# A new order table for a fused attention and gated-MLP kernel: the second batch in bf16, constants on GpSimd, more unread matmuls, more crossings by DMA

## The chip, the cores and the metric

The kernel runs on one core of one Trainium2 chip. The metric is device microseconds of one execution. The core has five engines, each with its own queue that it works off in order: PE (TensorE: matmuls and transposes, results in the eight banks of PSUM), DVE (VectorE), ACT (ScalarE), POOL (GpSimd) and SP (SyncE, which here only issues DMAs). ACT and POOL issue DMAs too; POOL's are written by its software and can change the type on the way, SP's and ACT's are not.

## The reference

Two stages. First a linear attention over q, k, v of 8 batches x 8 heads x 576 tokens x 64, with a feature map of 2 x 128 features; then a gated MLP (512 to 1024, halved, mixed over the tokens, back to 512) over the attention's output.

```python
def phi(x):
    proj = np.einsum('bhsd,df->bhsf', x, w_phi)
    proj = proj - np.max(np.abs(proj), axis=-1, keepdims=True)
    return np.concatenate([np.exp(proj), np.exp(-proj)], axis=-1)
q_p, k_p = (phi(q), phi(k))
kv = np.einsum('bhsf,bhsd->bhfd', k_p, v)
z = np.sum(k_p, axis=2)
num = np.einsum('bhsf,bhfd->bhsd', q_p, kv)
den = np.einsum('bhsf,bhf->bhs', q_p, z)[..., None] + 1e-06
return (num / den).astype(np.float32)
...
h = np.maximum(x @ w_in, 0.0)
u, v = (h[..., :d_ff // 2].copy(), h[..., d_ff // 2:].copy())
v_n = (v - mu) / np.sqrt(var + 1e-06)
v_s = np.einsum('ts,bsd->btd', w_spatial, v_n) + b_spatial[None, :, None]
gated = u * v_s
return (gated @ w_out).astype(np.float32)
```

## The kernel before

The 576 tokens of a batch are four blocks of 128 and a tail of 64. The tails of two batches make one tile of 128, so there are eight batches and four groups of tails (group g holds batches 2g and 2g+1).

The order of all work is one long string, `ORDER`. A word such as `tk.1.0.1:0` or `vs.0.0.0:0@V` names an operation and its numbers (batch, half of the heads or block, part), behind the colon the PSUM banks or buffers it takes, and behind the @ the engine (A for ACT, V for DVE, P for POOL, S for SP; the words of PE have none). A loop at the kernel's end reads the words and issues each as it comes; nothing is reordered afterwards. Each engine so gets its words in the string's order, and an instruction waits only for what it reads and for buffers to come free.

The operations that matter here:

- `lkf`, `lqf` (batch 0) and `lkg`, `lqg` (batch 1) load k and q as fp32 into buffers that other tiles use later (`ob`, `uT`, `vn`, `xT`), issued on ACT or SP. `lk`, `lq` load later batches into `ld` as bf16, issued on POOL. `lkt`, `lqt` load a group's tails as fp32 into `tf` on SP, and `ckt`, `cqt` cast them on POOL into `tl`; `lkb`, `lqb` load them as bf16 on POOL.
- `tk`, `tq` turn four 128 x 128 blocks of k or q on PE (line 505), and `tkc`, `tqc` copy the result from PSUM to `T`. Later batches cross by `xk`, `xq`, a DMA transpose on SP (line 488). Tails: `tkt`, `tqt` on PE (line 549) and `xkt`, `xqt` by DMA (line 536).
- `kp`, `qp` are projections (line 574), `km`, `qm` their maxima over the features on DVE (line 579), `ke` the exponentials of k on ACT (line 583), `kem`, `kemw` those of its maxima (line 588), `vs`, `vst` the products of v with them (lines 629 and 641), `kv` the products of keys and values on PE (lines 659 and 661).
- The maxima of q have to be subtracted along the other axis. `qs` splits them into two bf16 parts on POOL (lines 674 and 675, into `mhl`), and they cross either by `qt`, a transpose on PE (line 679), and the copy `qc`, or by `qd`, a DMA transpose on SP (line 725). `qf` reads them (`mT`, line 689) and `qe` takes the exponential (line 694).
- `warm` is a number of matmuls of the identity with itself whose result nobody reads (line 361).
- `cident2`, `csel`, `csel2`, `chalf`, `zmhl`, `zvnt` set up constants: the bf16 identity, a selector, an exponent, cleared or filled buffers.
- The MLP: `vm`, `vr`, `vb`, `va`, `vw`, `vn` (lines 849 to 875), `um`, `ur` (line 917), `sm`, `sg` (lines 931 to 940), `om`, `oc`, `od` (line 946, a copy from PSUM to `ob`, and the output's DMA on SP). `omh`, `och`, `odh` do one output tile in two halves (line 965).

```python
def qd(e, b, cc, hg):
    nc.sync.dma_start_transpose(out=get("mT", (b, cc, hg)), in_=at["mhl", (b, cc, hg)])
...
def lk(e, b):
    nc.gpsimd.dma_start(out=get("ld", ("k", b)), in_=main_ap(k, b, 0, H))
...
def warm(e, n):
    place = places.pop(0)
    for i in range(n):
        nc.tensor.matmul(out=bank(place)[:, 3 * P:4 * P], lhsT=ident, rhs=ident, start=True, stop=True)
```

In `turn`, which `tk` and `tq` call, a batch that has no `ld` buffer is turned from its fp32 tile with the fp32 identity, and one that has is turned in bf16.

## Time and profile before

| | us |
|---|---|
| three runs | 267.02, 266.33, 265.49 |
| their median | 266.33 |
| the profiled execution | 267.15 |
| its span, first to last instruction | 265.4 |
| PE busy | 246.8 |
| DVE busy | 218.5 |
| ACT busy | 197.8 |
| POOL busy | 177.8 |

The profile names each group of instructions by line, engine, operation, and output and input tiles. Matmuls are pipelined: one of 128 columns lasts about 0.22 us, while several in a row start far closer together, so a short gap between two matmuls can hide in the busy time. Some matmul records can be missing. PEclk is the clock that the chip grants PE, in tenths or as a share of the full one. A wait names the engine, the line that waited, and what came last before it could go on. POOL's instructions that issue DMAs stand in its queue like others.

### The profile page before, as it was taken

What the parts mean: (1) busy time and instruction counts of PE and PEld (TensorE: products, weight loads), DVE (VectorE), ACT (ScalarE), POOL (GpSimd) and SP (SyncE); (2) the same over time, 40 slices, a digit from 0 to 9 for tenths busy, and PEclk for the clock granted to TensorE, in tenths of its full rate; (3) what the DMA queues carried; (4) which work ended last, traced back from release to release, by engine and by line L of the source; (5) the groups of instructions that cost most, each with busy time, mean ns of one, the idle gap of its engine ahead of it and who ended that gap; (6) DMA issues with size and microseconds to landing.
All of it is one profiled execution on the core that took longest, in us unless ns stands there. A gap on an engine that the chain in (4) does not pass through costs nothing. (4 is left out here: it accounts for less than half of the span.)

```text
span 265.4 us, 8226 instructions
## 1 busy us (share of the span) xinstructions
PE 246.8 (93%) x3305; PEld 156.5 (59%) x3341; DVE 218.5 (82%) x371; ACT 197.8 (75%) x319; POOL 177.8 (67%) x322
## 2 busy tenths in 40 slices
PE   4787799999999999999999989999999999999993
PEld 4666577756555567465556656455546665546441
DVE  4799969998799999998999958999998768594550
ACT  2799669999979999989898778898779736412033
POOL 4029989699999983879999891269988911556000
PEclk9999869999999999999999999999999999999999
DMA  6999999993699969899999899896900670003546
GB/s 174 343 287 290 218 194 211 239 102 22 125 235 191 159 159 168 221 190 141 188 179 247 134 146 210 172 155 145 308 23 0 86 166 2 1 2 132 149 143 212
DMA packets 82682, 42.92 MB, mean 162 GB/s; under 512 B 51538, under 2 KB 78034, under 8 KB 82644
## 3 DMA queue, kind: packets, MB, share of 16 engines
q1 hardware_dynamic: 61700, 30.98, 53.7%
q0 software_dynamic: 18512, 9.05, 27.7%
q10 hardware_dynamic: 2432, 2.36, 2.9%
q8 instruction: 26, 0.43, 0.6%
q14 instruction: 12, 0.10, 0.1%
HBM read 32.82 MB, written 9.44 MB: 159 GB/s over the span
## 5 line engine op out<-in xcount | busy, mean ns | idle before, releaser
L694 ACT ACTIVATE qf<-banks 128x1024 bf16<-128x1024 f32 x72 | 70.4, 1027 | 9.3 <-PE banks L689 8.3
L629 POOL TENSOR_TENSOR vs<-v,em 128x512 bf16<-128x512 f32 x61 | 63.2, 1052 | 7.2 <-ACT em L588 6.8
L583 ACT ACTIVATE kf<-banks 128x1024 bf16<-128x1024 f32 x64 | 63.7, 1042 | 4.1 <-PE banks L574 1.8
L579 DVE TENSOR_REDUCE mq<-banks 128x8 f32<-128x1024 f32 x36 | 43.4, 1216 | 3.4 <-PE banks L574 2.7
L579 DVE TENSOR_REDUCE mk<-banks 128x8 f32<-128x1024 f32 x32 | 38.6, 1213 | 1.2 <-PE banks L574 0.7
L917 PE MATMUL banks<-xT,w_u 128*128 128x512 bf16 x128 | 32.4, 379 | 0.1
L931 PE MATMUL banks<-w_spT,vn 128*128 128x512 bf16 x117 | 31.7, 379 | 0.7 <-issue 0.2
L849 PE MATMUL banks<-w_v,xT 128*128 128x512 bf16 x116 | 31.3, 379 | 0.7
L273 ACT COPY ob<-banks 128x512 f32<-128x512 f32 (+1 forms) x25 | 14.3, 591 | 21.5 <-PE banks L946 21.5
L946 PE MATMUL banks<-w_out,uT 128*128 128x512 bf16 x114 | 29.6, 379 | 0.5 <-issue 0.2
L940 DVE TENSOR_TENSOR uT<-banks,uT 128x512 bf16<-128x512 f32 x32 | 21.5, 682 | 7.4 <-PE banks L933 7.3
L279 ACT ACTIVATE vr<-banks 128x512 bf16<-128x512 f32 (+1 forms) x28 | 16.8, 606 | 11.4 <-PE banks L849 9.6
L659 PE MATMUL banks<-vs,kf 128*128 128x66 bf16 x512 | 24.5, 194 | 0.9 <-POOL vs L629 0.8
L859 POOL TENSOR_SCALAR vn<-vr,mv,rs 128x512 bf16<-128x512 bf16 x32 | 24.4, 772 | 0.9
L659 PEld LDWEIGHTS <-kf 128*128 128x128 bf16 x512 | 22.1, 98 | 4.8 <-issue 2.3
L755 DVE TENSOR_TENSOR x<-banks,rc 128x512 bf16<-128x512 f32 x32 | 22.1, 690 | 1.2 <-DVE rc L750 0.2
L574 PE MATMUL banks<-wphi,T 64*128 64x128 bf16 x512 | 22.4, 217 | 0.5 <-ACT tT L273 0.2
L871 DVE BATCH_NORM_STATS2 st<-vr 128x6 f32<-128x512 bf16 x32 | 21.4, 683 | 1.5 <-ACT vr L279 1.2
L661 PE MATMUL banks<-vst,kft 128*128 128x66 bf16 x128 | 21.3, 192 | 1.3 <-POOL vst L641 1.3
L744 PEld LDWEIGHTS <-qf 128*128 128x128 bf16 x512 | 19.0, 97 | 4.4 <-issue 0.8
L744 PE MATMUL banks<-kv,qf 128*128 128x66 bf16 x512 | 20.9, 193 | 0.3 <-DVE mq L579 0.2
L574 PEld LDWEIGHTS <-T 64*128 64x128 bf16 x512 | 15.6, 94 | 7.6 <-issue 5.8
(131 smaller groups left out, 470.5 us busy)
## 6 DMA issues: line engine op xcount, KB each, us to landing
v<-in_v_dram SPq DMA_DIRECT2D x16, 512.0 KB, 5.1
out_dram<-ob SPq DMA_DIRECT2D x31, 256.0 KB, 2.9
ld<-in_q_dram POOLq DMA_DIRECT2D x6, 512.0 KB, 8.1
ld<-in_k_dram POOLq DMA_DIRECT2D x6, 512.0 KB, 8.2
ob<-in_k_dram ACTq DMA_DIRECT2D x4, 256.0 KB, 4.6
uT<-in_q_dram ACTq DMA_DIRECT2D x2, 512.0 KB, 10.4
vn<-in_k_dram SPq DMA_DIRECT2D x2, 512.0 KB, 8.3
vt<-in_v_dram SPq DMA_DIRECT2D x8, 128.0 KB, 7.3
```

The costliest lines, as they stand in the source:

```text
L574: nc.tensor.matmul(out=bank(banks[y])[:, n * F:(n + 1) * F], lhsT=xT[halves[y], n, :], rhs=wphi[halves[y], :], start=True, stop=True)
L579: nc.vector.tensor_reduce(out=out_, in_=pp.rearrange("p y (n f) -> p y n f", f=F), axis=AX.X, op=ALU.max, apply_absolute_value=True)
L583: nc.scalar.activation(out=kf[:, s].rearrange("p y n f -> p y (n f)"), in_=pp, func=AF.Exp, bias=0.0, scale=(1.0, -1.0)[s])
L629: ENG[e].tensor_tensor(out=get("vs", (b, j))[:, s, :, 0:D], in0=at["v", (b, j // 2)][:, (j % 2) * n:(j % 2 + 1) * n, :], in1=at["em", (b, ...
L659: nc.tensor.matmul(out=pv[:, hh, s, :], lhsT=kf[:, s, c % 2, 2 * hh + c // 2, :], rhs=w[:, s, NB * hh + c, :], start=(c == 0), stop=False)
L694: nc.scalar.activation(out=at["qf", u][:, s].rearrange("p y n t -> p y (n t)"), in_=at["pq", u], func=AF.Exp, bias=0.0, scale=(1.0, -1.0)[s])
L744: nc.tensor.matmul(out=at["pn", u][:, y, n, :], lhsT=f[:, s, y, n, :], rhs=at["kv", b][:, hg * HH + n, s, :], start=(s == 0), stop=(s == 1))
L849: nc.tensor.matmul(out=bank(place)[r], lhsT=lhs[:, kc, r], rhs=w_v[:, kc, :], start=(kc == 0), stop=(kc == KC - 1))
L859: ENG[e].tensor_scalar(out=out_, in0=in_, scalar1=mv, scalar2=rs, op0=ALU.add, op1=ALU.mult)
L917: nc.tensor.matmul(out=bank(place).rearrange("p (c t) -> p c t", c=NB), lhsT=w_u[:, kc, dc * P:(dc + 1) * P], rhs=at["xT", b][:, :, kc, :] ...
L931: nc.tensor.matmul(out=bank(place), lhsT=at["vn", b][:, c, cs], rhs=w_spT[:, c, 0:T0], start=(c == 0), stop=False)
L946: nc.tensor.matmul(out=bank(place), lhsT=at["uT", b][:, dc, c * P:(c + 1) * P], rhs=w_out[:, dc, :], start=(dc == 0), stop=(dc == KC - 1))
```

## The change

The string is another one. It has 1436 words for 1417, and almost none stands where it stood. What differs beside the order:

- Batch 1's k and q are loaded as bf16 by POOL (`lk.1`, `lq.1` for `lkg`, `lqg`), so that their 32 transposes on PE are of bf16. Batch 0 stays fp32.
- The tails of group 1 are loaded as bf16 by POOL (`lkb.1`, `lqb.1` for `lkt.1`, `lqt.1`, `ckt.1`, `cqt.1`) and cross by DMA (`xkt.1`, `xqt.1`), as groups 2 and 3 did; group 0 stays on PE.
- The maxima of batches 2 and 3 cross by DMA (eight `qd` for eight `qt` and eight `qc`), as those of batches 4 to 7 did.
- `cident2`, `csel`, `csel2`, `chalf` and two `zmhl` move from DVE to POOL, one `zvnt` to POOL and one to ACT. Three `vs` move from DVE to POOL. Copies from PSUM are dealt out anew between ACT and DVE, among them 15 `ur`.
- 233 unread matmuls in 43 words for 95 in 10: 28 of the words are of five: 25 stand among the first batches' work and three at the very end.
- On SP the bias `lbs` and the first tail of k are issued first, and one quarter of batch 0's k (`lkf.2`) moves there from ACT.
- The last output tile is a whole one (`om.7.0`); the tile in halves stands before it.

```diff
 ORDER = """
-cident@P lphi@S lkf.3:1@A zvst.0@P cident2@V warm.21:0 zmhl.0@V lqt.0:0@S csel@V lkf.0:3@A chalf@V csel2@V lkf.1:0@A
-zmhl.3@V zmhl.2@P zmhl.1@P lqf.0:1@A lkg.0:0@S lkg.1:1@S lkf.2:2@A lkt.0:1@S tk.0.1.1:4 warm.3:0 lqf.1:0@A tk.0.0.0:5
-warm.4:0 ctab@A tkc.0.0.0:1@V tk.0.0.1:6 warm.9:0 tkc.0.0.1@A cphi@V kp.0.0:0,1 tkc.0.1.1:0@A kp.0.1:2,3 ke.0.0.1:0@A
-km.0.1:0@V kp.0.3:6,7 tq.0.0.0:4 warm.10:5 ke.0.0.0@A km.0.3:1@V lvt.0:0@S ke.0.1.0:1@A tk.0.1.0:5 tqc.0.0.0:2@V
-lv.0.0:0@S ke.0.1.1@A tkc.0.1.0@V tq.0.0.1:4 warm.5:5 km.0.0@V tqc.0.0.1@A ke.0.3.0:2@A lqg.1:0@S qp.0.0.0:2,3
-kp.0.2:4,5 qm.0.0.0:3@V tk.1.0.1:0 ke.0.3.1@A tq.0.1.0:1 tkc.1.0.1:1@V tqc.0.1.0:0@A tq.0.1.1:2 lqg.0:1@S tk.1.0.0:3
...
-qr.1.1.0:1@V lv.4.0:3@S qx.1.1.0@V lk.4:1@P qt.2.0.1:2 vm.1.0:7 vrt.0.1:0@A txc.1.1@V vs.2.1.1:3@P vbt.0.1:3@V
...
-sm.7.1:5 sg.6.3@V sg.6.1@V sm.7.0:2 sg.7.1@V om.6.0:5 sg.7.0@V sg.7.3@V om.6.1:1 oc.6.0:2@A od.6.0@S om.7.2:7
-oc.6.1:1@A od.6.1@S omh.7.3.0:3 oc.7.2:3@A om.7.0:6 och.7.3.0:0@V od.7.2@S odh.7.3.0@A om.6.3:7 oc.7.0:4@A om.6.2:4
-od.7.0@S oc.6.3:2@A od.6.3@S om.7.1:1 oc.6.2:1@A od.6.2@S omh.7.3.1 oc.7.1:3@A och.7.3.1@A od.7.1@S odh.7.3.1@A
+cident@P lbs:0@S lkf.0:0@A cident2@P warm.23:0 lphi@S chalf@P zmhl.2@P ctab@A zmhl.3@P zmhl.0@P lkt.0:1@S zsp@P
+zmhl.1@P lk.1:0@P lkf.2:4@S lkf.1:2@A lvt.0:0@S lkf.3:1@A zvnt.0@P tk.0.0.0:4 warm.3:0 lqf.0:1@A lv.0.0:3@S warm.5:7
+warm.1:0 tkc.0.0.0:0@V zvnt.1@A warm.5:2 warm.3:0 csel@P cphi@V warm.5:7 warm.7:0 spb@P kp.0.0:6,7 warm.5:4
+ke.0.0.1:0@A tk.0.0.1:3 warm.15:0 tkc.0.0.1@V ke.0.0.0@A warm.5:3 warm.5:0 lqf.1:2@A km.0.0:0@V tk.0.1.1:1 warm.5:0
+warm.5:4 tkc.0.1.1:1@V warm.5:2 kp.0.1:4,5 ckt.0:0@P kp.0.3:6,7 warm.5:3 km.0.1@V lv.0.1:1@S ke.0.3.1:2@A zvst.0@P
+tkt.0:3 warm.5:2 warm.5:2 tktc.0:0@A km.0.3:1@V warm.5:0 warm.5:1 ke.0.1.0:1@A tk.0.1.0:1 csel2@P tq.0.0.0:3 lqt.0:0@S
+ke.0.3.0@A tkc.0.1.0@V lq.1:1@P tq.0.0.1:2 warm.5:0 tqc.0.0.0:2@V tqc.0.0.1@A tk.1.0.0:7 lsp:0@P tk.1.1.0:3
+kem.0.1:0@A tkc.1.0.0:3@V kem.0.0@A tk.1.1.1:2 lspt:1@P ke.0.1.1@A tkc.1.1.0:5@V tk.1.0.1:0 qp.0.1.0:6,7 warm.5:1
+tkc.1.0.1@V lq.2:2@P qm.0.1.0:2@V tkc.1.1.1@A kp.0.2:0,1 tq.0.1.0:4 ke.0.2.1:3@A vsz.0.0:0@P lk.2:0@P warm.5:5
+tqc.0.1.0:4@V qp.0.0.0:6,7 warm.5:3 ke.0.2.0@A lv.1.0:2@S qm.0.0.0:1@V qs.0.1.0:0@P kpt.0:4,5 lv.1.1:0@S lin.0@P
...
+qd.2.1.0:2@S qf.1.1.0:6,7 qe.1.1.1.0:3@A txc.1.0:1@V vn.0.3@P kp.2.1:2,3 sm.0.1:0 km.2.1@V qd.2.0.1:1@S qe.1.1.1.1@A
...
+oc.7.2:4@A od.7.2@S om.5.3:0 oc.5.1:1@A od.5.1@S om.6.1:7 oc.5.3:0@V om.6.3:6 od.5.3@S oc.6.1:2@A od.6.1@S om.7.1:1
+oc.6.3:3@A od.6.3@S omh.7.3.0:4 oc.7.1:4@V om.5.0:0 och.7.3.0:1@A od.7.1@S odh.7.3.0@A omh.7.3.1 oc.5.0:0@A om.5.2:2
+och.7.3.1@V od.5.0@S odh.7.3.1@A om.7.0:0 oc.5.2:2@A warm.5:5 od.5.2@S oc.7.0:3@A warm.5:7 warm.5:6 od.7.0@S
 """
...
     @op
     def csel(e):
-        nc.vector.tensor_tensor(out=sel1, in0=ident.rearrange("p (a x) -> p a x", a=2)[:, :, 0:HH],
-                                in1=ident.rearrange("p (a x) -> p a x", a=2)[:, :, HH:2 * HH], op=ALU.add)
-        nc.vector.tensor_tensor(out=sel1[:, 0, :], in0=sel1[:, 0, :], in1=sel1[:, 1, :], op=ALU.add)
+        ENG[e].tensor_tensor(out=sel1, in0=ident.rearrange("p (a x) -> p a x", a=2)[:, :, 0:HH],
+                              in1=ident.rearrange("p (a x) -> p a x", a=2)[:, :, HH:2 * HH], op=ALU.add)
+        ENG[e].tensor_tensor(out=sel1[:, 0, :], in0=sel1[:, 0, :], in1=sel1[:, 1, :], op=ALU.add)
```

The beginning of POOL's queue, of before, from its first memset to the second load (`tl` and `tf` are tails, `mhl` the split maxima, `ld` the bf16 loads):

```order
L346 MEMSET vst_101 128x2112
L342 MEMSET mhl_111 128x128
L342 MEMSET mhl_110 128x128
L275 CAST tl_76<-tf_78 128x512
L674 CAST mhl_109<-mq_106 128x2x4
L675 TENSOR_TENSOR mhl_109<-mq_106,mhl_109 128x2x4
L441 DMA ob_166<-in_moe_w_spatial_dram 64x576
L436 DMA vn_156<-in_moe_w_spatial_dram 128x2304
L398 DMA ld_62<-in_q_dram 128x8x256
L394 DMA ld_63<-in_k_dram 128x8x256
```

and of the change, from the load of batch 1's k to the first split (`sel` is the selector, `vnt` and `w_spT` are buffers of the MLP):

```order
L395 DMA ld_62<-in_k_dram 128x8x256
...
L276 CAST tl_76<-tf_78 128x512
L347 MEMSET vst_101 128x2112
L330 TENSOR_SCALAR sel<-sel_175 128x512
L399 DMA ld_63<-in_q_dram 128x8x256
L437 DMA vn_154<-in_moe_w_spatial_dram 128x2304
L442 DMA ob_165<-in_moe_w_spatial_dram 64x576
L399 DMA ld_64<-in_q_dram 128x8x256
L276 CAST vs_97<-em_92 128x16x2
L395 DMA ld_62<-in_k_dram 128x8x256
L675 CAST mhl_109<-mq_107 128x2x4
```

The loads of batch 1 (`ld_62`, `ld_63`) now stand in this queue, the second behind the cast of the first tail; batch 2's load into `ld_62`, which waits until PE has turned batch 1's k out of it, stands ahead of the first split.

PE's queue where batch 1's k is turned, of before (`vn_154` holds half of that k as fp32, `uT_159` half of batch 0's q):

```order
L574 LDWEIGHTS T_65
L574 MATMUL banks<-wphi,T_65 128x128
L505 MATMUL banks<-ident_f,vn_154 128x128 x4
L505 MATMUL banks<-ident_f,uT_159 128x128 x8
L505 MATMUL banks<-ident_f,vn_154 128x128 x4
L574 LDWEIGHTS T_67
L574 MATMUL banks<-wphi,T_67 128x128
```

and of the change (`ob_168` and `uT_160` are of batch 0):

```order
L506 MATMUL banks<-ident_f,ob_168 128x128 x4
L506 MATMUL banks<-ident_f,uT_160 128x128 x8
L362 LDWEIGHTS ident
L362 MATMUL banks<-ident 128x128
...
L506 LDWEIGHTS ld_62
L506 MATMUL banks<-ident,ld_62 128x128
...
L575 LDWEIGHTS T_67
L575 MATMUL banks<-wphi,T_67 128x128
```

All sixteen transposes of that k now stand together, behind a block of five unread matmuls, and read the bf16 load.

SP's queue behind the second batch's v, of before (`T` and `tT` are turned k, q and tails):

```order
L488 DMA_TRANSPOSE T_69<-ld_64 128x8x128
L488 DMA_TRANSPOSE T_71<-ld_62 128x8x128
L488 DMA_TRANSPOSE T_70<-ld_64 128x8x128
L536 DMA_TRANSPOSE tT_79<-tl_76 128x4x128
L488 DMA_TRANSPOSE T_65<-ld_62 128x8x128
```

and of the change:

```order
L489 DMA_TRANSPOSE T_69<-ld_63 128x8x128
L726 DMA_TRANSPOSE mT_115<-mhl_109 128x128
L726 DMA_TRANSPOSE mT_114<-mhl_110 128x128
L489 DMA_TRANSPOSE T_65<-ld_63 128x8x128
L489 DMA_TRANSPOSE T_71<-ld_64 128x8x128
L489 DMA_TRANSPOSE T_68<-ld_64 128x8x128
L726 DMA_TRANSPOSE mT_113<-mhl_109 128x128
```

The crossings of batch 2's maxima (`mT` from `mhl`) now stand between those of batch 3's k and q; before, they were on PE.

## The prediction

> **What bounds the kernel now.** The page's shares of busy time come first, then the waits of TensorE (PE), the busy time by stage with the granted clock, and the timeline where these point.

> ```profile
> span 265.4 us, 8226 instructions
> ...
> PE 246.8 (93%) x3305; PEld 156.5 (59%) x3341; DVE 218.5 (82%) x371; ACT 197.8 (75%) x319; POOL 177.8 (67%) x322
> ```

> PE is busy for 93% of the span and the next engine for 82%. The two lists below are PE's waits from 0 to 60 us and from 60 to 262 us: sum, number of times, longest.

> ```profile
> PE banks L361 <- DVE mhl L342: 3.5, 1, 3.5
> PE banks L679 <- POOL mhl L675: 1.4, 3, 0.7
> PE banks L661 <- POOL vst L641: 1.3, 1, 1.3
> PE banks L505 <- DMA ob<-in_k_dram: 0.6, 1, 0.6
> PE banks L659 <- POOL vs L629: 0.5, 1, 0.5
> PE banks L505 <- DMA uT<-in_q_dram: 0.5, 1, 0.5
> PE banks L361 <- DVE T L275: 0.3, 1, 0.3
> PE banks L744 <- DVE mq L579: 0.2, 1, 0.2
> PE banks L574 <- DVE mq L579: 0.2, 1, 0.2
> ```

> ```profile
> PE banks L689 <- DMA mT<-mhl: 1.3, 1, 1.3
> PE banks L679 <- POOL mhl L675: 0.7, 1, 0.7
> PE banks L659 <- POOL vs L629: 0.3, 1, 0.3
> ```

> After 60 us the named waits come to 2.3 us in 202; from there PE runs its queue without a stop, and the end comes when it has worked it off. Before 60 us the waits are 8.5 us, 3.5 of them ahead of the first matmul and 5.0 later. Busy time by stage shows one more loss (columns: stretch, its length, then each engine's busy time, the granted TensorE clock, the DMA share).

> ```profile
> core 0: us, PE busy (x) PEld busy (x) DVE busy (x) ACT busy (x) POOL busy (x), PEclk, DMA share, GB/s
> 22.00:24.00 2.00, 0.76 (x8) 0.32 (x5) 2.00 (x4) 2.00 (x7) 1.75 (x7) 1.00 1.19 302
> ...
> 26.00:28.00 2.00, 0.82 (x17) 0.72 (x15) 2.00 (x3) 1.28 (x2) 1.86 (x4) 1.00 1.07 182
> ...
> 30.50:37.40 6.90, 6.90 (x56) 4.85 (x52) 5.69 (x9) 4.02 (x6) 5.99 (x9) 0.51 1.29 214
> ```

> In two 2 us slices PE is busy for 0.76 and 0.82, and right after them the clock is granted at 0.51 for 6.9 us, in which PE has no idle time. So the kernel is bound by PE's queue, and what a change is worth is what it takes from PE's lost time in the first 40 us, or from the queue itself.

> **The change, part by part.** The sum goes against the profiled execution, 267.15 us (span 265.4 and 1.75 around it), 0.8 above the median of 266.33. Each term is carried over to the median.

> *The clock.* The added unread matmuls stand in blocks of three to five between the first batch's operations. If they keep the clock up, the 6.9 us shrink to what the engines need at full clock: PE 6.90 x 0.51 = 3.5 us. VectorE (DVE) was busy there for 5.69 us, of which one operation leaves it:

> ```profile
> 31.80 1.69 DVE L275 COPY vnt<-ident 128x512 bf16<-128x512 bf16 x2
> ```

> 5.69 - 1.69 = 4.0 us is then the longer of the two, and I take 6.9 - 4.0 = **-2.9 us**. The bounds are -3.4 (PE alone) and -1.2 (DVE keeps its 5.69).
> [...]

> *The second batch in bf16.* Its 32 transposes of q and k change from fp32 to bf16. Four of fp32 at full clock and a row of unread bf16 matmuls of the same shape:

> ```profile
> 20.81 0.66 PE L505 MATMUL banks<-ident_f,vn 128*128 128x128 f32 x4
> 21.31 1.00 PE L361 MATMUL banks<-ident 128*128 128x128 bf16 x15
> ...
> 40.32 0.40 PE L505 MATMUL banks<-ident,ld 128*128 128x128 bf16 x4
> ```

> The fp32 group holds PE from 20.81 to 21.31, 0.50 us. A bf16 matmul lasts 0.22 us, but the row of 15 starts one every (1.00 - 0.22)/14 = 0.056, so four are 0.22; the four bf16 transposes at 40.32 last 0.40, which is 0.22 + 3 x 0.06. Eight groups save 8 x (0.50 - 0.22) = **-2.2 us**. Bounds: 0 if PE only waits longer for the loads, -2.2 if it doesn't wait.

> *Crossings by DMA.* Eight transposes of maxima (batches 2 and 3) and eight of the second group's tails leave PE: 16 x 0.056 = 0.9. One wait of 0.7 on POOL (GpSimd) goes too, and in its place the eight new readers wait for a DMA. Of the 16 such DMAs now, issued on SP at about 1.2 us each, one made PE wait, for 1.3 (both rows above):

> ```profile
> L725 SPq DMA_TRANSPOSE mT<-mhl x16: 1093/1166/1533, 117.4 to 211.3; - x16
> ...
> DMA to landing us min/median/max: 2.2/3.5/6.6
> ```

> Half as many again, 0.65 expected, against the 0.7 that goes: **-0.9 us**. Bounds: -1.6 without a new wait, +1.0 with two of 1.3. SP's own added issue time, ten crossings by 1.2, is covered by its queue being ahead of its readers: a crossing lands 3.5 us after its issue, and in the new order the readers stand tens of operations behind. The copies that go from DVE and ScalarE (ACT) cost those engines nothing that PE waits for.

> *Unread matmuls.* 95 become 233. Of the 138 added, 15 stand behind the last product and delay nothing on PE; 2 are in the first row, which starts earlier. The other 121 take 121 x 0.056 = 6.8 us if PE has work that they hold up, and 0 if they fall into waits. The waits after the start are 5.0 us in the list to 60 us. I take the part that cannot fit: **+1.8 us**. Bounds 0 and +6.8.

> *Constants and products on POOL.* The bf16 identity was cast on DVE while POOL set memory:

> ```profile
> 1.33 2.14 DVE L275 CAST ident<-ident_f 128x128 bf16<-128x128 f32 x1 [1.33 <-POOL ident_f masks.py:199]
> ```

> PE's first row could begin some 1.6 us sooner with a short cast on POOL (2.14 less half a microsecond, an estimate), but the first real transposes need the first piece of k, which takes 4.6 us to land:

> ```profile
> ob<-in_k_dram ACTq DMA_DIRECT2D x4, 256.0 KB, 4.6
> ```

> I count 0 (bounds -0.3 and 0). Three products of DVE's go to POOL, 1.05 us each by POOL's own, ahead of the first key-value product; in exchange POOL no longer stands where it stood longest:

> ```profile
> L629 POOL TENSOR_TENSOR vs<-v,em 128x512 bf16<-128x512 f32 x61 | 63.2, 1052 | 7.2 <-ACT em L588 6.8
> ```

> ```profile
> POOL tl L275 <- DMA tf<-in_k_dram: 13.0, 1, 13.0
> ...
> 18.48 0.19 POOL L674 CAST mhl<-mq 128x8 bf16<-128x8 f32 x1 [1.51 <-DVE mq L579]
> ```

> The loads of that tail are now issued third on SP, where they were issued after two loads of 512 KB. I take the 13.0 us that come free as enough for the constants, the load issues and the three products (3.2 us) that now stand there, so 0; what it costs if that cover is gone is the slower rival.

> *The end.* The last output was written in halves, now it is whole:

> ```profile
> 260.82 0.42 issue
> 261.24 0.38 ACT ob L273
> ```

> ```profile
> out_dram<-ob SPq DMA_DIRECT2D x31, 256.0 KB, 2.9
> ...
> out_dram<-ob ACTq DMA_DIRECT2D x2, 128.0 KB, 2.5
> ```

> The copy takes 0.59 (the row of whole copies, mean 591 ns, below) for 0.38 and the transfer 2.9 for 2.5: **+0.6 us**, bounds 0 and +0.6.

> ```profile
> L273 ACT COPY ob<-banks 128x512 f32<-128x512 f32 (+1 forms) x25 | 14.3, 591 | 21.5 <-PE banks L946 21.5
> ```

> Sum: -2.9 - 2.2 - 0.9 + 1.8 + 0.6 = -3.6. The profiled time becomes 263.5 and the median **262.7 us**.

> **The rivals.** *The clock drops all the same.* [...] For it: the waits of 0.7 and 1.3 us on POOL each outlast a block. Against it: the blocks stand at about 30 places before 45 us. The term of 2.9 is lost: 262.7 + 2.9 = 265.6, no change that can be told.

> *The second batch's loads are late.* k and q of batch 1 now go through POOL's queue and not SP's. What both kinds took from 0 to 30 us (to landing, last column):

> ```profile
> vn<-in_k_dram SPq DMA_DIRECT2D x2, 512.0 KB, 8.3
> xT<-in_q_dram SPq DMA_DIRECT2D x2, 512.0 KB, 6.8
> ...
> ld<-in_q_dram POOLq DMA_DIRECT2D x1, 512.0 KB, 13.6
> ld<-in_k_dram POOLq DMA_DIRECT2D x1, 512.0 KB, 17.0
> ```

> POOL issues the load of k behind its first constants, which ended at 3.4 us before (rows below); at 17.0 it lands at 20.4, where the old transposes of this batch began at 14.5. PE's queue then stands for 5.9 us with everything behind it, and so does POOL, whose next load into the same buffer stands ahead of the first split. 262.7 + 5.9 = 268.6 us, slower. It decides from a landing at 14.5 on, and has cost the gain of 3.6 at about 18. Against it: the two slow loads stand behind the split at 18.48, so with far more traffic ahead of them than at 3.4.

> ```profile
> 3.04 0.35 POOL L342 MEMSET mhl<- 128x128 bf16 x2
> ```

> ```profile
> 14.48 0.65 PE L505 MATMUL banks<-ident_f,vn 128*128 128x128 f32 x4
> ```

> [...]

> *More than the sum.* If every block fills a wait, the clock is held at PE's bound, and nothing is lost at the end: 262.7 - 1.8 - 0.5 - 0.6 - 0.3 = 259.5, and down to 258 where POOL's earlier start takes the 1.3 us wait away too.

> **How the numbers follow.** 0.5% of 266.33 is 1.3 us, which is about what can be told from no change. I give the forecast 0.57, the clock's drop 0.15, late loads 0.16, and more than the sum 0.12. The first lies in 260 to 265.5, nearly all of it faster. Faster: 0.54 + 0.12 and a little of the second, 0.67; same: 0.17; slower: 0.16. For 8 in 10 the range leaves out the end of the late loads and a little below: 257.8 to 268.0 us.

> **What would show it.** Right: PEclk stays at 9 in the slices from 26 to 40 us, the second batch's transposes start by 15 us with no wait on their load, and PE's waits before 60 us are below 3 us beside the blocks. Wrong: a wait of PE's transposes on DMA of over 3 us, a stretch at half clock, several waits of line 690 on a crossing, or useful matmuls that stand behind a block with operands long there. If PE is seen waiting after 60 us for more than 4 us in all, the order itself and not one of these steps is the cause.

## The result, and the profile after

The changed kernel takes 280.42 us (median of four executions, 279.65 to 281.97), the kernel before beside it 266.67: a ratio of 1.0527, 95% interval 1.0467 to 1.0588. The forecast was 262.7 with a range of 257.8 to 268.0. Sign and size are wrong. (All medians here are over every execution of a kernel; some executions of the same kernel are some per cent longer than its others, and a ratio leaves out, on both sides, those over 1.5% above the fastest.)

The profiled execution took 279.65 us. The page of the changed kernel, in the same rows as before:

```profile
span 277.8 us, 8460 instructions
...
PE 251.3 (90%) x3429; PEld 162.9 (59%) x3463; DVE 208.2 (75%) x354; ACT 196.9 (71%) x315; POOL 186.1 (67%) x337
...
PEclk9877799999999999999999999999999999999999
```

PE is busy for 251.3 us where it was 246.8, and idle for the other 26.5 us of its span where it was 18.6: these 4.5 and 7.9 us are the whole difference of the spans, 277.8 - 265.4 = 12.4. PE's waits from 0 to 60 us, and below them from 60 us to the end (sum, times, longest):

```profile
PE banks L506 <- DMA uT<-in_q_dram: 5.8, 1, 5.8
PE banks L506 <- DMA ob<-in_k_dram: 3.5, 1, 3.5
PE banks L362 <- POOL neghalf L335: 1.7, 1, 1.7
...
PE banks L850 <- DVE mq L580: 2.2, 1, 2.2
PE banks L850 <- DMA xT<-x: 1.9, 1, 1.9
PE banks L850 <- DMA xTt<-xt: 1.8, 1, 1.8
PE banks L690 <- DMA mT<-mhl: 0.6, 1, 0.6
```

The first list sums to 12.1 us (8.5 before), the second, with its small rows, to about 8 (2.3 before). The busy time by stage, in the prediction's columns, shows the clock twice at half:

```profile
11.20:18.00 6.80, 5.38 (x52) 4.92 (x53) 1.92 (x2) 0.81 (x1) 4.22 (x5) 0.50 1.21 300
...
24.90:31.70 6.80, 3.13 (x30) 2.46 (x30) 1.62 (x2) 0.00 (x0) 0.00 (x0) 0.50 1.22 255
```

This loss must not be added to the waits, for it overlaps them: PE's wait of 5.8 us ends at 28.57, and the clock is at half from 24.86 on, so PE works in only 3.13 us of the second stretch, and in 5.38 of the first. At half clock work takes longer: four fp32 transposes (line 506) last 1.09 us at 28.57 and 0.60 us at 7.03, where the granted clock is full. If half of PE's busy time there is lost, that is about 2.7 + 1.6 = 4.3 us, against 6.9 / 2 = 3.4 before, an estimate.

Where the longest wait came from is in the chain of waits from 0 to 42 us (start, length, what):

```profile
4.72 11.97 DMA vt<-in_v_dram
16.69 0.02 issue
16.71 11.72 DMA uT<-in_q_dram
28.43 0.14 issue
28.57 1.09 PE banks L506 x4
```

and in ACT's timeline:

```profile
6.05 0.37 ACTq L383 DMA_DIRECT2D uT<-in_q_dram  x1
...
16.71 0.38 ACTq L383 DMA_DIRECT2D uT<-in_q_dram  x1
17.19 1.02 ACT L584 ACTIVATE kf<-banks 128x1024 bf16<-128x1024 f32 x1 [7.75 <-DVE mk L580]
```

The second half of batch 0's q (`lqf.1`) was issued at 16.71; before, at 4.27. ACT reached it at 9.4 us and stood in front of it until the second load of v's tail, a transfer that has nothing to do with it, had landed at 16.69. Two rows of the changed program say why. Both instructions use and wait on the same semaphore of finished DMAs:

```
ACT  L383 DMA uT_161<-in_q_dram 128x4x256 [waits DMAHW0_49]
SP   L290 DMA vt_80<-in_v_dram 64x8x64 [waits DMAHW0_49]
```

In the changed kernel's trace SP's and ACT's 140 DMAs use eight such semaphores (DMAHW0 to 7), so 132 of them follow another DMA on their own. None of the 132 was issued before that one had landed, and eight were issued 0.02 us after its landing, `lqf.1` among them. So the sentence on the kernel before that an instruction waits only for what it reads and for buffers is not the whole of it: here a DMA issue also waited for its semaphore. The issuing engine's queue then stood with its own work behind it, ACT's from 9.4 to 16.71 us.

The wait of 3.5 us for k is of the same kind. It is for the quarter `lkf.3`. In the kernel before this was ACT's first load, issued at 0.73 us; now it is the third, issued at 4.53, and its semaphore was last used by the load of the projection (`lphi`), issued at 1.40 and landed 3.1 us later, at 4.51.

After 60 us, VectorE's and SP's timelines show what caused the 2.2 us of line 850:

```profile
91.95 0.69 DVE L276 COPY ob<-banks 128x512 f32<-128x512 f32 x1 [2.33 <-DMA out_dram<-ob]
```

```profile
86.16 0.37 SPq L958 DMA_DIRECT2D out_dram<-ob  x1
```

The copy of output tile 0.2 takes the buffer that tile 0.3 has just left, and that tile's output, issued at 86.16, has not landed. The other two waits are crossings of x, which the chain of waits shows at 8 to 9 us from issue to landing (of the eight crossings of batches' x between 60 and 200 us the median is 3.9 us and the longest 8.9; before, 4.1 and 7.0):

```profile
112.11 8.87 DMA xT<-x
...
173.96 8.41 DMA xTt<-xt
```

One part went as forecast: all 16 bf16 transposes of batch 1's k in one go, without a wait.

```profile
20.59 1.08 PE L506 MATMUL banks<-ident,ld 128*128 128x128 bf16 x16
```

### The profile page after: what moved, and what is told of

It reads as the page before. It is cut to its first block, busy times and chain, and to the rows that moved or that the text cites. A ratio compares the mean times of both kernels' runs of the same rounds, so it can differ in the third digit from the quotient of the medians.

```text
span 277.8 us, 8460 instructions
## 1 busy us (share of the span) xinstructions
PE 251.3 (90%) x3429; PEld 162.9 (59%) x3463; DVE 208.2 (75%) x354; ACT 196.9 (71%) x315; POOL 186.1 (67%) x337
## 3 DMA queue, kind: packets, MB, share of 16 engines
q0 software_dynamic: 22704, 10.36, 31.7%
## 4 chain that ended last, share of the span: by engine, by line
PE 52%; DMA 18%; POOL 11%; DVE 7%; ACT 5%; issue 3%; SPq 1%; POOLq 0%; DVEq 0%; ACTq 0%
PE banks L850 7%; PE banks L918 7%; PE banks L947 6%; PE banks L932 6%; DMA vt<-in_v_dram 4%; DMA uT<-in_q_dram 4%; POOL vs L630 4%; PE banks L660 4%; PE banks L575 4%; DMA xT<-x 3%; PE banks L745 3%; DMA xTt<-xt 3%; DMA mT<-mhl 2%; PE banks L686 2%; DVE mq L580 2%
## 5 line engine op out<-in xcount | busy, mean ns | idle before, releaser
L630 POOL TENSOR_TENSOR vs<-v,em 128x512 bf16<-128x512 f32 x64 | 65.7, 1040 | 7.7 <-DMA v<-in_v_dram 4.8
L850 PE MATMUL banks<-w_v,xT 128*128 128x512 bf16 x116 | 30.6, 380 | 4.8 <-DVE mq L580 2.2
L947 PE MATMUL banks<-w_out,uT 128*128 128x512 bf16 x114 | 29.0, 379 | 0.8 <-issue 0.5
L274 ACT COPY ob<-banks 128x512 f32<-128x512 f32 (+1 forms) x21 | 12.2, 582 | 18.5 <-PE banks L947 16.4
L280 ACT ACTIVATE vr<-banks 128x512 bf16<-128x512 f32 (+1 forms) x25 | 15.1, 604 | 12.9 <-PE banks L850 5.5
L660 PE MATMUL banks<-vs,kf 128*128 128x66 bf16 x512 | 23.7, 194 | 0.2
L362 PE MATMUL banks<-ident 128*128 128x128 bf16 x233 | 20.2, 244 | 1.7 <-POOL neghalf L335 1.7
L642 POOL TENSOR_TENSOR vst<-vt,emt 64x512 bf16<-64x512 f32 x16 | 16.6, 1038 | 7.4 <-ACT emt L589 6.8
## 6 DMA issues: line engine op xcount, KB each, us to landing
v<-in_v_dram SPq DMA_DIRECT2D x16, 512.0 KB, 5.6
out_dram<-ob SPq DMA_DIRECT2D x31, 256.0 KB, 3.0
ld<-in_k_dram POOLq DMA_DIRECT2D x7, 512.0 KB, 9.3
ld<-in_q_dram POOLq DMA_DIRECT2D x7, 512.0 KB, 11.9
vt<-in_v_dram SPq DMA_DIRECT2D x8, 128.0 KB, 6.2
uT<-in_q_dram ACTq DMA_DIRECT2D x2, 512.0 KB, 11.1
out_dram<-ob SPq DMA_DIRECT2D x8, 128.0 KB, 6.2
ob<-in_k_dram ACTq DMA_DIRECT2D x3, 256.0 KB, 5.5
```

Of the source, the lines that this page charges most:

```text
L630: ENG[e].tensor_tensor(out=get("vs", (b, j))[:, s, :, 0:D], in0=at["v", (b, j // 2)][:, (j % 2) * n:(j % 2 + 1) * n, :], in1=at["em", (b, ...
L660: nc.tensor.matmul(out=pv[:, hh, s, :], lhsT=kf[:, s, c % 2, 2 * hh + c // 2, :], rhs=w[:, s, NB * hh + c, :], start=(c == 0), stop=False)
L850: nc.tensor.matmul(out=bank(place)[r], lhsT=lhs[:, kc, r], rhs=w_v[:, kc, :], start=(kc == 0), stop=(kc == KC - 1))
L947: nc.tensor.matmul(out=bank(place), lhsT=at["uT", b][:, dc, c * P:(c + 1) * P], rhs=w_out[:, dc, :], start=(dc == 0), stop=(dc == KC - 1))
```

## The experiments

Theories: **A**, the loads of batch 0 stand in the wrong places of ACT's and SP's queues, above all `lqf.1`; **B**, the unread matmuls hold PE up; **C**, the loads are late by traffic, in whatever order; **D**, crossings by DMA and SP's queue are late; **E**, the order itself: what is gained is waited for at the next place; **F**, the output buffer. The edits are of the changed kernel's order unless another is named; each run stands beside executions of the kernel before on the same chip (medians 265.7 to 267.0).

### The late load of q

```diff
 e1_lqf_first
-lqf.0:1@A lv.0.0:3@S ... warm.5:0 lqf.1:2@A km.0.0:0@V
+lqf.0:1@A lqf.1:2@A lv.0.0:3@S ... warm.5:0 km.0.0:0@V
 e2_lane
-lk.1:0@P lkf.2:4@S lkf.1:2@A lvt.0:0@S
+lk.1:0@P lvt.0:0@S lkf.2:4@S lkf.1:2@A
```

> One word of the changed kernel moves: the load of the second half of batch 0's q is issued on ACT right behind that of the first half, ahead of ACT's first copy and exponentials. Theory A (that load stood in ACT's queue from 9.4 to 16.7 us until an unrelated load, the second tail of v, had landed, and came 12 us later still): it is issued by about 6.5 us and lands by 18, PE's wait of 5.85 us on it goes and with it the half clock from 24.9 to 31.7 us (6.83 us at half speed, some 3 us), 280.4 - 5.9 - 3 = 271.5, range 269 to 275. Rival B (the unread matmuls hold PE up): 279 to 281. Rival E (the order itself: what is gained at 28 us is waited for again at the next place): above 277.

Measured: 275.72 us (271.39 to 278.04), a little above the range. `lqf.1` is issued by 10.6 us, and PE's wait for it is gone. But a wait of 4.3 us for `lkf.3` remains, whose issue on ACT again follows the landing of the projection's load (chain of waits):

```profile
1.42 3.57 DMA wphi_f<-in_w_phi_dram
4.99 0.02 issue
5.01 9.32 DMA ob<-in_k_dram
```

And from 86.0 us PE stood 2.9 us for the output buffer, with half clock from 88.2 on:

```profile
88.00:95.00 7.00, 5.72 (x42) 2.84 (x43) 5.02 (x9) 3.80 (x5) 2.94 (x8) 0.51 1.32 215
```

So A holds for its wait, and part of its gain was given back at the next place: 0.7 us more of wait than before the edit, and by the same estimate half of 5.72 us, 2.9, by the clock.

> Two neighbouring words of SP are swapped: the two loads of v's first tail go ahead of the third quarter of k. ACT's order stays, the late load of q too. If the wait is for whichever load last used the same completion semaphore (theory A), the late load now waits for the quarter of k, which lands at about 10 to 11 us and not at 16.7: it is issued some 6 us earlier, PE's wait of 5.85 us mostly goes, 272 to 276. If the wait is one on ACT's place in the order or on a full queue, nothing changes: 279 to 282.

Measured: 279.84 us, ratio 1.0456 (1.0332 to 1.058). The time missed the forecast, the mechanism did not. With ACT's order untouched, the load is issued at the landing of the transfer that now holds its semaphore (chain of waits):

```profile
4.76 9.09 DMA ob<-in_k_dram
13.85 0.02 issue
13.87 9.33 DMA uT<-in_q_dram
```

The quarter of k landed later than assumed (13.85), so the load was issued only 2.8 us sooner. Neither a place in ACT's queue nor a full queue would give this equality of 13.85 and 13.87.

The same load, issued late in the kernel before, with nothing of the change:

```diff
 e11_before_late_q (of the kernel before)
-tk.0.0.0:5 ... lqf.1:0@A ... ke.0.1.1@A
+... ke.0.1.1@A lqf.1:0@A
```

> The kernel before with one word moved: the load of the second half of batch 0's q stands behind ACT's third exponential, so it is issued at about 13 us and not at 4.3. Nothing of the change is in it. Theory A (this load alone makes most of the loss): PE stands some 6 to 8 us for it ahead of 30 us and may lose clock after it, 271 to 276. If the change's loss needs the other edits: 266 to 268.

Measured: 273.86 us, 1.0302 (1.0246 to 1.0358), 7.4 us from one word. The load is issued at 14.51 us and not at 4.27. This shows what its lateness costs; that a semaphore made it late in the changed kernel is shown above. PE's wait and the clock, in the longest of the five executions (277.82 us):

```profile
PE banks L505 <- DMA uT<-in_q_dram: 5.9, 2, 4.7
```

```profile
PEclk9975999999999999999999968999999999999999
```

### Unread matmuls and crossings of maxima

e3 leaves out the 29 words `warm.5:*`, 26 of them ahead of the end (the section on the change counts 28 and 25). e4 replaces the eight `qd.2.*` and `qd.3.*` by `qt` and `qc` (for instance `qd.2.1.0:2@S` by `qt.2.1.0:1` and `qc.2.1.0:2@V` some 25 words later).

> Left out: all 29 unread matmul words of five (145 matmuls; the result is the same). Rival B (they hold PE's useful work up): 126 of them ahead of the end, 126 x 0.056 = 7 us less, 273 to 275, with PE's waits for loads no longer. Theory A: they stand inside waits that stay, 279 to 282, and PE's named waits in the first 30 us grow by what the blocks filled. If the blocks do hold the clock up, there is more half clock than the two stretches of 6.83 us: 281 to 285.

Measured: 281.05 us, 1.0487 (1.0351 to 1.0624). B falls as the cause of the loss: 145 matmuls fewer, and no time won. But two effects meet here. PE is busy for 246.5 us, 4.8 less, while its waits before 60 us grow (6.3 for `lqf.1`, and new ones of 1.8 and 1.3 on ACT) and the clock is at half for 10.2, 6.8 and 3.4 us instead of 6.8 twice. So the matmuls stood mostly inside waits, and in this profile the clock was at half for longer without them (mean clock of the four executions 0.955 to 0.973, for 0.967 to 0.979 with them).

> Undone: the eight crossings of the maxima of batches 2 and 3 by DMA; they are turned by PE again and copied by VectorE, tens of words ahead of their readers. Rival D (the added DMAs make SP's queue and the transfers late, which PE pays with its waits of 1.8 to 2.0 us at 91, 119, 164 and 180 us): those waits go, 274 to 277. Theory A (the front alone): 8 x 0.056 = 0.5 more on PE and 8 copies on VectorE, 280 to 282.

Measured: 280.64 us, 1.0575 (1.0485 to 1.0664). In its profile the wait on xT is gone, that on xTt is still 2.1 us, and PE waits 0.8 and 0.4 us for VectorE at the new transposes. D falls as the cause of the loss: undoing this part wins nothing that can be told from the interval.

### The output buffer

In e5, `ob` buffers 0 and 3 are exchanged from `oc.0.2` on (`oc.0.2:3@V` becomes `oc.0.2:0@V`, `oc.1.2:0@A` becomes `oc.1.2:3@A`, and so on); e6 adds the edit of e1.

> Only buffer numbers of `ob` change: from the copy of output tile 0.2 on, buffers 0 and 3 are exchanged, so that this copy no longer takes the buffer that tile 0.3 has just left. Theory F (VectorE's queue stood from 89.5 to 91.9 us because that buffer's output DMA, issued at 86.2, had not landed, and PE's line 850 behind it): the stand goes, PE's wait of 2.2 us at 91 us with it, 280.4 - 2.4 = 278.0. Rival D (SP's queue and the traffic are late as such): the copy still waits for a DMA or PE waits as long within 10 us after: 280 to 281. In both the front stays as it was: PE's wait of about 6 us for the second half of q.

Measured: 280.26 us, 1.052 (1.0434 to 1.0606). The wait at 91 us is gone, but the next in line, for a crossing of x, has grown and is followed by half clock. Alone, the edit is worth nothing:

```profile
PE banks L850 <- DMA xT<-x: 3.1, 1, 3.1
```

> The edits of e1_lqf_first and of e5_ob together. In e1_lqf_first PE stood 3.0 us at the same copy (85.7 to 88.9 us) and was at half clock afterwards from 88 to 95 us: 40 to 50 us of useful work took 17.6 us there, 11.5 in the kernel before. Theory A with F: both go, 275.7 - 6 = 269.7, range 267.5 to 272. Rival E (the order itself, what is gained is waited for at the next place): above 273.

Measured: 270.38 us, 1.0132 (1.0045 to 1.022). Alone, the edits bring the ratio from 1.053 to about 1.03 (e1, from only two executions, 274.72 and 271.39 us) and to 1.052 (e5); together they bring it to 1.013. That is more than their sum, though e1's two executions leave the size open. The profiles show why: in e1 the wait at the buffer grew, in e5 the wait for x. Now ACT's two loads of q end their issue at 11.2, because `lqf.1` waits for a quarter of k (landed at 10.78):

```profile
6.06 5.11 ACTq L383 DMA_DIRECT2D uT<-in_q_dram  x2
```

### The other loads of batch 0, and the crossings of x

e7, e9: all k and q loads first, in two ways; e8: e7 with later readers; e10: e9 with x turned by PE.

```diff
 e7_front (of e6)
+cident@P lkf.0:0@A lkf.1:2@A lqf.0:1@A lqf.1:2@A ... lphi@S lkf.3:1@S lkf.2:4@S lkt.0:1@S lbs:0@S ... lv.0.1:1@S lvt.0:0@S ... lspt:1@P spb@P
 e8_front_late_readers (of e7)
-vm.2.1:4 ... vr.2.1:4@V ... qp.4.1.0:0,1 ... vmt.1.2:0 ... kv.4.0:2
+qp.4.1.0:0,1 vm.2.1:4 vr.2.1:4@V ... kv.4.0:2 vmt.1.2:0 vrt.1.2:3@V umt.1:1 vbt.1.2:0@V
 e9_front2 (of e6)
+lbs:0@S lkf.0:0@A lkf.1:2@A ... lphi@S ... lqf.0:1@A lqf.1:2@A ctab@A ... lkt.0:1@S ... lkf.3:1@S lkf.2:4@S ... lv.0.1:1@S lvt.0:0@S
 e10_turn_x (of e9)
-xx.2.0:1@S ... xx.2.1@S ... xxt.1:1@S
+tx.2.0:5 txc.2.0:1@V tx.2.1:0 txc.2.1@V tx.2.3:1 txc.2.3@A tx.2.2:4 txc.2.2@A txt.1.2:4 txtc.1.2:1@V
```

> As e6_lqf_ob, and the loads of batch 0 go out first: all four quarters of k and both halves of q as the first loads of ACT and SP, the tail of k, the bias and the tail of v behind them. Theory A (what the new order loses ahead of 45 us is late loads): PE's wait of 4.3 us for the third quarter of k goes too, kv's first product starts at about 26 to 29 us and not at 32; e6_lqf_ob less 3 to 4: 264 to 268. Rival C (the loads are late because of the traffic of batch 1's and 2's loads, not of their place): the wait moves to another load, within 1.5 us of e6_lqf_ob.

Measured: 272.01 us, 1.0238 (1.0153 to 1.0324): a miss. The waits for k were gone, but k's tail now came late and POOL, which stood for it, held PE twice (2.7 and 2.9 us). C's words ("the wait moves to another load") are what happened, at 1.6 us above e6.

> As e7_front, and two readers of crossings by DMA stand later: the product of block 2.1 (line 850) by three PE words, the product of the tails of group 1 by three, each with what reads it. Their waits in the changed kernel were 1.9 (xT, 8.9 us from issue to landing) and 1.8 us (xTt, 8.4 us). If these waits set the end (theory D in its small form): 1 to 2.5 us below e7_front. If other waits take their place: within 0.7 of it.

Measured: 276.61 us, 1.0366 (1.0278 to 1.0455): a miss. One of the two readers was the wrong one (the late tails were group 2's, not group 1's), and a wait of 3.3 us for a crossing of batch 4 (`T`) came up instead.

> As e6_lqf_ob (270.4), with the two queues of batch 0's loads sorted by who reads first, the tails of k left early: SP issues the bias, the projection, the tail of k and then the third and the second quarter of k; ACT the first and the other quarter of k, then both halves of q, ahead of its table load; v's tail behind v. In e6_lqf_ob ACT still stood until 10.8 us, when the quarter of k that had used the same completion semaphore landed, and PE waited 1.6 us for k and 2.1 us behind it. Theory A: these go, 266 to 268.5. Rival C (with all loads early the traffic makes another one late, as in e7_front): within 1.5 of 270.4.

Measured: 273.04 us, 1.0264 (1.0211 to 1.0318): a miss. The quarter `lkf.3`, now issued on SP at 4.2 us and beside 1 MB of q, still cost 2.0 us, and the crossing `T` 4.3 at 105 us.

> As e9_front2, and x of batch 2 and the tails' x of group 1 are turned by PE (five times four matmuls, copies on VectorE and ACT) where three DMAs crossed them. PE's waits for those DMAs were 2.6 and 2.6 us in e6_lqf_ob, 2.8 and 2.2 in e7_front, and a half clock of 3.4 us followed one of them. Theory D in its small form (three crossings whose readers stand too close): the waits go for 5 x 0.22 = 1.1 us of PE, 3 to 5 us below e9_front2. If other waits take their place (rival E): within 1.5 of it.

Measured: 271.72 us, 1.0184 (1.0103 to 1.0265). That is 1.3 us below e9, within the 1.5 that its rival gave. No wait on xT any more; 2.2 us on xTt remained, again because the wrong group had been turned.

Then the tails of the right group (e12: `txt.2.2:2 txtc.2.2:0@V` for `xxt.2:0@S`), and k ahead of q:

```diff
 e13_k_first (of e12)
+lkf.0:0@A lkf.1:2@A lkf.3:1@A ... lkf.2:4@A lqf.0:1@A lqf.1:2@A ctab@A
 e14_k_first_q_later (of e12)
+lkf.0:0@A lkf.1:2@A lkf.3:1@A ... ctab@A lqf.0:1@A lqf.1:2@A ... lkf.2:4@S
```

> As e10_turn_x, and the tails' x of group 2 are turned by PE too (the wait of 2.2 us for xTt that was left at 169 us was theirs, not group 1's). Theory D in its small form: that wait goes, 271.7 - 2 = 269.5, 267 to 270.5. Rival E (another wait takes its place): 271 to 273.

Measured: 270.77 us, 1.014 (1.0036 to 1.0244). The wait on xTt is gone. In the profiled execution, a long one (275.42 us), the wait for k was 4.8 us and that for `T` 4.0.

> As e12_turn_tails, and ACT issues all four quarters of k first and the halves of q behind them, which wait for completion semaphores of early loads. Theory A (the loads' order): the wait of 3.0 us for the third quarter of k goes, and the half clock of 3.4 us after it, e12_turn_tails less 3 to 4: 265 to 267. Rival C (traffic, some load is late in any order): within 1.5 of e12_turn_tails.

> As e13_k_first, but the second quarter of k stays on SP behind the tail, and the halves of q are issued behind ACT's table load, a little later. Theory A: as e13_k_first or 0.5 us better where the tail of k lands sooner, 264.5 to 267. Rival C: within 1.5 of e12_turn_tails.

Measured: 266.54 us (264.32 to 273.71), 0.9981 (0.9933 to 1.0029), and 266.07 us (263.64 to 272.67), 0.9961 (0.9915 to 1.0007). The whole loss is won back. What is left at 15 us is the prediction's own rival, batch 1's k through POOL (e14, waits and chain of waits):

```profile
PE banks L507 <- DMA ld<-in_k_dram: 3.4, 1, 3.4
```

```profile
3.20 15.46 DMA ld<-in_k_dram
```

### What was left

```diff
 e15_k1_earlier (of e14)
-chalf@P zmhl.2@P ... zmhl.1@P lk.1:0@P
+chalf@P lk.1:0@P zmhl.2@P ... zmhl.1@P
 e16_k1_v_later (of e15)
-lv.0.0:3@S ... lv.0.1:1@S
+ke.0.0.0@A lv.0.0:3@A lv.0.1:1@A
 e18_crossing_earlier (of e15)
-xq.5.1:1@S ... lvt.2:0@S ... qd.3.0.0:2@S ... xq.4.0:2@S
+xq.5.1:1@S xq.4.0:2@S ... qd.3.0.0:2@S lvt.2:0@S
```

> As e14_k_first_q_later (266.1), with POOL's load of batch 1's k moved ahead of its clearing of buffers: issued at about 1.7 and not 3.2 us. In e14 it took 15.5 us to land and PE waited 3.4 us for it. If the issue decides: it lands 1.5 us sooner, 264.6, range 263.5 to 265.5. If the traffic decides (what is issued beside it shares the same transfer engines): it lands as late as before, within 0.7 of 266.1.

Measured: three executions at 262.97 to 263.45 us and three at 268.52 to 270.00 (the median between them, 265.98, is of no use; the first three give a ratio of 0.9894, 0.9847 to 0.9941). The wait for batch 1's k is gone: issued at 1.6 us, it had landed when PE came to it at 16.7, where it landed at 18.7 in e14. So the issue decided. The profiled execution is one of the longer ones; PE waits 4.1 us in it for the crossing of batch 4's q, which its chain of waits shows:

```profile
98.67 7.95 DMA T<-ld
```

> As e15_k1_earlier, with the two loads of batch 0's v (512 KB each) moved from SP, which issued them at 4 to 5 us, to ACT behind its second exponential, at about 9 us. If the traffic beside it makes batch 1's k late: 1 MB less ahead of it, it lands by 15 us, PE's wait of 3.4 us and the half clock of 3.4 us behind it go, 262.5, range 261 to 264.5. If then v is late in its place (needed from 23 us on): 265 to 267.

Measured: 270.31 us, 1.0139 (1.0091 to 1.0187): a miss, and the first fault over again. In ACT's queue, v's loads waited for the semaphores of v's tail (chain of waits of its longest execution, 276.17 us):

```profile
4.11 12.68 DMA vt<-in_v_dram
16.80 0.02 issue
16.82 0.37 ACTq L404
```

> As e14_k_first_q_later, without the 29 unread matmul words of five (145 matmuls). In e3_no_blocks, with late loads everywhere, they made no difference. By the prediction's terms: up to 6.8 us less where they hold work up (its value was 1.8), up to 3 us more where the clock falls for want of them. If both hold, 264 to 269; more half clock than the one stretch of 3.4 us in the granted clock would show the second, useful matmuls behind blocks the first.

Measured: 267.76 us, 0.9999 (0.9959 to 1.0038), beside 0.9961 with the blocks: unclear in time. In the stage from 13 to 24 us (e14 with blocks first, then e17 without) the granted clock differs, in one profiled execution each:

```profile
13.00:24.00 11.00, 7.58 (x97) 6.22 (x94) 5.89 (x9) 6.66 (x13) 5.55 (x10) 0.84 1.25 239
```

```profile
13.00:24.00 11.00, 6.88 (x61) 5.38 (x61) 6.03 (x9) 6.72 (x12) 4.68 (x9) 0.53 1.26 233
```

The clock is short of full by 11 x 0.16 = 1.8 us with blocks and by 11 x 0.47 = 5.2 without; what of it falls into PE's waits is not lost to PE. Over all executions the mean granted clock is 0.981 to 1.000 with blocks (ten, median 0.997) and 0.962 to 0.994 without (twelve, median 0.974).

> As e15_k1_earlier, with the crossing of batch 4's first half of q ahead of an output, a crossing of maxima and the two loads of v's third tail on SP (issued some 4 us sooner), and those loads behind the crossing of maxima. If this crossing makes the difference between the executions of 263 and of 269 us: none above 266, median 262 to 264, faster than the kernel before by 1% or more. If the split has another cause: again about half of them at 268 to 270.

Measured: 263.42 us (262.49 to 266.49, twelve executions), ratio 0.9886 (0.985 to 0.9923). One execution is above the 266 that was expected as the limit. With one crossing moved ahead on SP the group near 269 us is gone; the three short executions of e15, on another chip, took as long as these. This version is 1.1% faster than the kernel before. Its page and PE's longest waits:

```profile
span 261.3 us, 8507 instructions
...
PE 249.6 (96%) x3453; PEld 162.4 (62%) x3487; DVE 210.4 (81%) x358; ACT 198.3 (76%) x317; POOL 186.2 (71%) x337
...
PEclk9999999999999999999999999999999999999999
```

```profile
PE banks L363 <- POOL neghalf L336: 1.7, 1, 1.7
PE banks L507 <- DMA ob<-in_k_dram: 0.5, 1, 0.5
```

## Why the prediction was wrong

**The step that failed** is a term that was put at nothing without a reason: the new places of batch 0's loads on ACT's and SP's queues. The prediction looks at these loads only where it reads "I count 0", under constants and products on POOL, and there it asks when the first piece of k lands and what POOL's queue has free. The order had moved v's tail, a quarter of k and the bias ahead of `lqf.1`, and `lkf.3` from ACT's first load to its third. The runs show in its place that `lqf.1` was issued at 16.71 us for 4.27, which made PE wait 5.8 us and brought the second stretch of half clock, and `lkf.3` at 4.53 for 0.73, with a wait of 3.5 us and the first stretch. A late `lqf.1` alone cost 7.4 us in the kernel before (e11). Repairing this load and the one buffer brought 280.4 to 270.4 (e6), the other loads and the crossings of x to 266.1 (e14).

**The clock**, -2.9: two stretches at half clock instead of none, about 4.3 us of loss by the estimate above. Each began inside a wait for a load, which the prediction did not have. That blocks keep the clock up has the clocks of e3 (mean 0.955 to 0.973 without them, 0.967 to 0.979 with them) and of e17 (0.53 from 13 to 24 us, where e14 has 0.84 with them) for it; that it saves time is not shown, since e17's time is within the interval. A second error sits in "each term is carried over to the median": of the seven executions of the kernel before beside e5 to e8, six ran at a mean clock of 0.999 to 1.000 and took 264.7 to 267.1 us. So the drop in the profiled execution (0.987) is not in most executions, nor in the median, and most of the 2.9 us was not there to be won. The length of a single wait did not tell whether the clock dropped: in the kernel before the longest wait in the 10 us ahead of the drop was 1.3 us, the changed kernel's two drops came inside waits of 3.5 and 5.8 us, and of e7's waits of 2.7, 2.9 and 2.8 us (from 12.7, 22.9 and 111.5 us) only the second had a drop behind it, at 27.33. The traces show what goes with a drop. Within each of the twenty, the clock changed only at multiples of 3.41 us from each other, and a drop went with PE's busy share of the stretch of 3.41 us just ahead of it. These are the stretches in which e7's three waits end; in the second alone PE is busy for less than half:

```profile
13.68:17.09 3.41, 1.73 (x28) 1.73 (x29) 0.93 (x1) 1.29 (x2) 2.39 (x3) 1.00 1.20 298
23.92:27.33 3.41, 1.55 (x22) 1.16 (x23) 1.28 (x3) 0.84 (x2) 3.23 (x9) 1.00 1.28 215
112.67:116.08 3.41, 1.84 (x23) 0.96 (x24) 0.69 (x1) 0.52 (x4) 0.00 (x0) 1.00 0.74 205
```

Counted over all twenty traces up to 255 us, the clock fell after 33 stretches at full clock: in 31 of them PE was busy for at most 0.48, in the other two for 0.54 (e11) and 0.56 (27.11 to 30.52 us, ahead of the drop in the kernel before). It stayed full after 1381, all but three of them busy for more than 0.50. It came back after 33 stretches, each busy for 0.90 or more. By this count, a wait in these traces went with a drop or not by how it lay against the stretches.

**The second batch in bf16**, -2.2: held. Sixteen transposes in 1.08 us against 16 x 0.50 / 4 = 2.0 is 1.8 us for the 32.

**Crossings by DMA**, -0.9: the waits for maxima after 60 us came to 0.6, less than the 1.3 before, to which 0.65 had been added, and turning them back changed nothing that can be told (e4). What was missed are crossings that the change did not add, of x: 1.9 and 1.8 us of waits, and 3.1 when something ahead of them was repaired. Their readers stand about as many PE words behind them as before (11 for 10 in batch 2, counted from its first crossing, 10 for 13 in the tails of group 2); the crossings landed later. Whether the added crossings on SP made them late stays half open: with those of maxima back on PE the wait on xT was gone, that on xTt was still 2.1 us (e4).

**Unread matmuls**, +1.8: no net time in e3 and e17, where the clock is lower without them; the term alone is not shown. **The end**, +0.6: from the last useful matmul to the end of the span it is 4.6 us, 4.3 before, so +0.3.

**The rivals.** "The clock drops all the same" was right that the term would be lost, not why: it has waits on POOL, and both stretches began inside waits for loads. "The second batch's loads are late" did not decide here, as PE came to them late enough, but its mechanism was real: 15.46 us to landing where 17.0 was taken, 3.4 us of PE in e14, gone in e15. None of the rivals had a load in ACT's queue. The last sentence of the prediction was right: more than 4 us of waits after 60 us (about 8) meant the order itself, and there these waits are a buffer taken too soon and crossings that landed late, the one hidden by the other (e5).

That e18 comes within 0.7 us of the forecast is not a confirmation of its sum: e18 has other loads first and six more turns on PE.

## What to carry to other kernels

Where a change moves words of an order, list each DMA issue on its engine with the semaphore it waits on and the transfer that used this semaphore last: here ACT, with its own work behind the issue, stood from 9.4 to 16.71 us until that stranger had landed. A load that is moved can also shift which semaphore the loads behind it get (e2: `lqf.1` then waited for a quarter of k, until 13.85, and no longer for v's tail). A wait that is taken away can come back at the next place (e5 alone: 280.26 us for 280.42, with e1's edit 270.38), so repair them together and read each trace for the next. A clock drop in one profiled execution belongs to that execution until the clocks of the others show it too (the kernel before: 0.987 in the profiled one, 0.999 to 1.000 in six of seven others).
